# Halved first loads, statistics summed in one piece and two queues for the last stores, in a kernel of linear attention and a gated feed-forward layer

## The chip, the cores and the metric

The kernel runs on one core of a Trainium2 chip. TensorE does the matrix products, VectorE (DVE) and ScalarE (ACT) the elementwise work, GpSimd (POOL) some elementwise work and the issue of the loads, SyncE (SP) the issue of most stores. The metric is the device time in microseconds (us); the span of a profile is 1.7 to 1.8 us shorter than the time of the same execution.

## The reference, cut to what matters

```python
kv  = einsum('bhsd,bhse->bhde', k, v)              # 8 batches, 8 heads, 576 rows, 64 columns
out = einsum('bhsd,bhde->bhse', q, kv)
x   = out / sqrt(mean(out*out, -1) + 1e-6) * g_norm    # then 4608 tokens x 512
h   = x @ w_in                                      # 512 x 1024
solu = h * softmax(h)
ln  = (solu - mean(solu)) / sqrt(var(solu) + 1e-6) * g_ln
y   = ln @ w_out                                    # 1024 x 512
```

## The kernel before

The 4608 tokens are worked in nine chunks of 512: the first 512 rows of each batch (chunks 0 to 7), and the last 64 rows of all eight (chunk 8, its q in the tile `q_last`). Each piece of work is put on a list with its engine, its length and a rank, and a greedy planner fixes the order in which the pieces are written out for each engine.

A chunk's way: load k, v, q; product k·v ("kv"), copied into the tile `kvd`; q turned by TensorE and copied; product q·kv ("o"); square, a product that sums over the heads ("s"), logarithm and exponential on ScalarE give x; then eight groups of four products with w_in ("h"), an exponential and a multiplication for each (`u = h * exp(h)`), and eight groups with w_out ("out"). The softmax's denominator cancels in the normalization, so three sums per token are enough: of u, of its square and of exp. TensorE forms them, VectorE turns them by a transpose, and a small product ("stat") puts them where they are used.

The loads of a chunk are whole, and twelve products on zeros keep TensorE busy before the first kv:

```python
plan.add("warm2", "pe", 2.6, -9.0, lambda: warm(12), [("qT_mm", 0, 1)], first=[("s", "warm2")])
...
def load_kv(name, src, b):
    t = T[name, b] = tile_of((name, b), [S // 6, H, 6, D], BF16)
    nc.gpsimd.dma_start(t.rearrange("p h i d -> p h (i d)"), src[b].rearrange("h (p i) d -> p h (i d)", i=6))
```

The sums are three pieces for the planner, with 32-column weights on a quarter of the array:

```python
def sums(c, part):
    ...
    for n in range(n_src):
        j = n % 4
        nc.tensor.matmul(T["sum", c][32 * j:32 * j + 32, :], stat_sel[:, i, :], src[:, n, :], ...,
                         tile_position=(0, 32 * j), ...)
...
for part in range(3):
    plan.add(("sums", c, part), "pe", (0.5, 0.5, 0.25)[part], r + 0.1 + 0.02 * part, ...)
```

Stores are issued by SyncE. Those of chunk 8 have the batch, 8, as the slowest dimension of what they write:

```python
def store(c, m):
    ...
        dst = out.rearrange("(b s) d -> b s d", b=B)[:, 512:S, :].rearrange("b (p j) d -> j b p d", j=4)
    nc.sync.dma_start(dst[j], T["ob", c, m][:, :])
```

The softmax here doesn't subtract the row's maximum and nothing guards it: scores larger than these inputs give would overflow.

Of the kernel before, what the change touches and what calls it, by code (L numbers as in the profile page):

```python
# [18 lines left out]
class Plan:  # L19
# [13 lines left out]
    def order(self):  # L33
        free, done, queue, lanes = {}, {}, 0.0, []
        held = {tag: [] for tag in self.bufs}
        waiting = {n: set(p[4]) for n, p in self.pieces.items()}
        behind = {}
        for n, needs in waiting.items():
            for m in needs:
                behind.setdefault(m, []).append(n)  # L40
        ready = [n for n, needs in waiting.items() if not needs]
        order = []
        while ready:
            best = None
            for n in ready:
                engine, length, rank, fn, needs, first, load = self.pieces[n]
                t = max([free.get(engine, 0.0)] + [done[m] for m in needs])
                for key in first:
                    old = held[key[0]]
                    if len(old) >= self.bufs[key[0]]:  # L50
                        last = self.users[old[-self.bufs[key[0]]]]
                        t = max([t] + [done.get(m, 1e9) for m in last])
                if load and len(lanes) >= 8:
                    t = max(t, lanes[-8])
                if t < 1e8 and (best is None or (t, rank) < best[:2]):
                    best = (t, rank, n)
            t, rank, n = best
            engine, length, rank, fn, needs, first, load = self.pieces[n]
            ready.remove(n)
            for key in first:  # L60
                held[key[0]].append(key)
            free[engine] = t + length
            done[n] = t + length + (0.2 if engine == "pe" else 0.12)
            if load:
                queue = max(queue, t + length + 1.0) + load
                done[n] = queue + 1.0
                lanes.append(done[n])
            order.append(fn)
            for m in behind.get(n, ()):
                waiting[m].discard(n)  # L70
                if not waiting[m]:
                    ready.append(m)
        assert len(order) == len(self.pieces)
        return order
# [3 lines left out]
def kernel(  # L78
# [33 lines left out]
    banks = {"h": 2, "out": 2, "o": 2, "s": 1, "misc": 1}  # L112
    bufs = {
        "k": 3, "v": 3, "q": 3, "qT": 4, "osq": 4, "lss": 2, "rst": 2, "oc": 2, "x": 2, "e": 4, "u": 2, "usq": 2, "es": 2,
# [43 lines left out]
    for i in range(3):  # L158
        nc.vector.memset(stat_sel[:, i, i:i + 1], 1.0 / 1024)

# [16 lines left out]
    plan.add("warm", "pe", 5.2, -9.0, lambda: warm(12), first=[("s", "warm")])  # L177
    for n, key in enumerate((("o_mm", 0, 1), ("s_mm", (0, 0, 0)), ("s_mm", (0, 1, 0)), ("s_mm", (0, 0, 1)), ("s_mm", (0, 1, 1)))):
        plan.add(("warm", n), "pe", 0.7, -9.0, lambda: warm(3, "misc"), [key], first=[("misc", "warm", n)])
    plan.add("warm2", "pe", 2.6, -9.0, lambda: warm(12), [("qT_mm", 0, 1)], first=[("s", "warm2")])  # L180
# [9 lines left out]
    plan.add("ident", "pool", 1.0, -1.75, make_ident)  # L190
# [3 lines left out]
    def load_kv(name, src, b):  # L194

        t = T[name, b] = tile_of((name, b), [S // 6, H, 6, D], BF16)
        nc.gpsimd.dma_start(t.rearrange("p h i d -> p h (i d)"), src[b].rearrange("h (p i) d -> p h (i d)", i=6))

    def load_q(b):
        t = T["q", b] = tile_of(("q", b), [128, H, 4, D], BF16)  # L200
        nc.gpsimd.dma_start(
            t.rearrange("p h j d -> p h (j d)"), q[b, :, 0:512, :].rearrange("h (p j) d -> p h (j d)", j=4)
# [15 lines left out]
    T["q", NC - 1] = q_last  # L218
    for b in range(B):
        at = b - 2.4 if b > 1 else (-2.0, -1.5)[b]  # L220
        behind = [] if b < 2 else [("x", (0, 1, 1))] if b == 2 else [("h_mm", b - 3, 2)]
        plan.add(("k", b), "pool", 0.75, at, lambda b=b: load_kv("k", k, b), behind, first=[("k", b)], load=3.0)
        plan.add(("v", b), "pool", 0.75, at + 0.01, lambda b=b: load_kv("v", v, b), behind, first=[("v", b)], load=3.0)
        plan.add(("q", b), "pool", 0.9, at + (0.1 if b else -0.1), lambda b=b: load_q(b), behind, first=[("q", b)], load=2.7)
        plan.add(("q_last", b), "pool", 0.6, 2.0 + 0.5 * b, lambda b=b: load_q_last(b),
                 [("h_mm", 2 + b // 2, 4 * (b % 2))], load=0.5)
    for half in range(2):
        plan.add(("w_in", half), "pool", 0.8, -1.8 + 0.01 * half, lambda half=half: load_w_in(half), load=2.7)
# [3 lines left out]
    def kv_mm(b):  # L232
        t = T["kv", b] = bank(("misc", "kv", b), [128, NP, D], FP32)
        for p in range(NP):
            for i in range(6):
                for hh in range(2):
                    h = 2 * p + hh
                    nc.tensor.matmul(  # L238
                        t[hh * 64:hh * 64 + 64, p, :], T["k", b][:, h, i, :], T["v", b][:, h, i, :],
                        start=(p == 0 and i == 0), stop=(i == 5), skip_group_check=True,  # L240
                    )

    def kv_copy(b, hh, z):

        dst, src = kvd[z * 64:z * 64 + 64, b, hh, :, :], T["kv", b][hh * 64:hh * 64 + 64, :, :]
# [13 lines left out]
    def qT_copy(c, hf):  # L259
        t = T["qT", c, hf] = tile_of(("qT", c, hf), [128, 4, 2, 128], BF16)  # L260
        nc.vector.tensor_copy(t[:, :, :, :], T["qTp", c, hf][:, :, :, :])  # L261

    def o_mm(c, hf, tag):
# [4 lines left out]
        for pp in range(2):  # L268
            for b in [c] if c < B else range(B):
                cols = slice(0, 128) if c < B else slice(16 * b, 16 * b + 16)  # L270
                for hh in range(2):
                    for z in range(2):
# [3 lines left out]
                            T["qT", c, hf][rows, 2 * pp + hh, :, cols], start=True, stop=True,  # L276
# [38 lines left out]
    for c in range(NC):  # L315

        r = {0: -1.7, 1: -0.9}.get(c, c - 1.6)
        w = {0: 0.7, 1: 0.8}.get(c, 1.0)
        if c < B:
            plan.add(("kv_mm", c), "pe", 1.15, r, lambda c=c: kv_mm(c), [("k", c), ("v", c)],  # L320
                     uses=[("k", c), ("v", c)], first=[("misc", "kv", c)])
            for hh in range(2):
                for z in range(2):
                    plan.add(("kv", c, hh, z), "act" if hh else "dve", 0.34, r + 0.05,
                             lambda c=c, hh=hh, z=z: kv_copy(c, hh, z), [("kv_mm", c)], uses=[("misc", "kv", c)])
        kvs = [("kv", b, hh, z) for b in ([c] if c < B else range(B)) for hh in range(2) for z in range(2)]
        for hf in range(2):
            loads = [("q", c)] if c < B else [("q_last", b) for b in range(B)]
            qtag = "h" if c == 0 and hf else "misc"
            plan.add(("qT_mm", c, hf), "pe", 0.5, (r + w * (0.1 + 0.1 * hf)) if c else -2.0, lambda c=c, hf=hf, tag=qtag: qT_mm(c, hf, tag),  # L330
                     ["ident", *loads], uses=[("q", c)] if c < B else [], first=[(qtag, "qT", c, hf)])
            plan.add(("qT", c, hf), "dve", 0.62, (r + w * (0.12 + 0.1 * hf)) if c else -2.0, lambda c=c, hf=hf: qT_copy(c, hf),
                     [("qT_mm", c, hf)], uses=[(qtag, "qT", c, hf)], first=[("qT", c, hf)])
            tag = "out" if c == 0 and hf else "o"
            plan.add(("o_mm", c, hf), "pe", 0.25 if c < B else 1.2, r + w * (0.35 + 0.5 * hf),
                     lambda c=c, hf=hf, tag=tag: o_mm(c, hf, tag), [("qT", c, hf), *kvs],
                     uses=[("qT", c, hf)], first=[(tag, c, hf, z) for z in range(2)])
# [112 lines left out]
    def stats(c):  # L450
        st = small.tile([128, 4, 3], FP32, name="st")
        nc.vector.tensor_copy(st[:, :, :], T["st", c][:, :, :])
        sq = small.tile([128, 4, 2], FP32, name="sq")
        nc.vector.tensor_tensor(out=sq[:, :, :], in0=st[:, :, 1:3], in1=st[:, :, 1:3], op=MUL)
        var = small.tile([128, 4], FP32, name="var")
        nc.vector.tensor_tensor(out=var[:, :], in0=st[:, :, 0], in1=sq[:, :, 0], op=SUB)
        T["vare", c] = small.tile([128, 4], FP32, name="vare")
        nc.vector.scalar_tensor_tensor(
            out=T["vare", c][:, :], in0=sq[:, :, 1], scalar=1e-6 * d_ff * d_ff, in1=var[:, :], op0=MUL, op1=ADD
        )  # L460
# [35 lines left out]
    def store(c, m):  # L496
# [5 lines left out]
        nc.sync.dma_start(dst[j], T["ob", c, m][:, :])  # L502

    for f in range(NF):
        plan.add(("w_mean", f), "pe", 0.25, 0.2 + 0.05 * f, lambda f=f: w_mean(f),
                 ["w_out", "g_mean"] + ([("w_mean", f - 1)] if f else []), uses=[] if f == 0 else [("out", "mean")],
# [3 lines left out]
    for c in range(NC):  # L510
        r = c + 1
        parts = [[("u", c, f) for f in range(NF)], [("usq", c, f) for f in range(NF)], [("es", c, n) for n in range(NF // 2)]]
        for part in range(3):
            plan.add(("sums", c, part), "pe", (0.5, 0.5, 0.25)[part], r + 0.1 + 0.02 * part,
                     lambda c=c, part=part: sums(c, part),
                     parts[part] + ((parts[1] + parts[2] if c < NC - 1 else []) if part == 0 else [("sums", c, part - 1)]),
                     uses=[(("u", "usq", "es")[part], c)] + ([("misc", "sum", c)] if part else []),
                     first=[] if part else [("misc", "sum", c)])
        plan.add(("turn", c), "dve", 0.62, r + 0.14, lambda c=c: sums_turn(c), [("sums", c, 2)],
# [5 lines left out]
        for m in range(4):  # L525
# [9 lines left out]
            plan.add(("store", c, m), "sp", 0.6, r + (2 * m + 3) / 8, lambda c=c, m=m: store(c, m),  # L535
# [34 lines left out]
```

## Time and profile before

| | before |
|---|---|
| time, first three runs | 223.78 us median (223.01 to 224.43) |
| the profiled execution | 220.5 us, span 218.7 us |
| kv of chunk 3 starts | 56.10 us |
| TensorE's last product ends | 207.68 us |
| span after it | 11.05 us |

The profiled execution is faster than each of the three timed ones. The page's row of the granted TensorE clock, in 40 slices of 5.5 us, in tenths:

```profile
PEclk9699999999999999999999999999999999999995
```

And two lines of TensorE's timeline at the start (start, length, line, operation, tile, shape, count, idle before and what ended it):

```profile
7.40 0.99 PE L257 MATMUL misc_ps<-ident,q_sb 128*128 128x128 bf16 x8 [2.04 <-DMA q_sb<-in_q_dram]
...
9.04 3.67 PE L175 MATMUL s_ps<-zeros 128*128 128x512 bf16 x12
```

TensorE waited 2.04 us for q, and then its clock was 0.5 from about 7.4 to 10.9 us. In this stretch it turns q and works through the twelve products on zeros, and then stands for v until 13.72. So here the slow stretch costs nothing.

### The profile page before, as it was taken

The numbers are of one execution on the slowest core, as the hardware profiler recorded it, in microseconds if no ns is written. First come the engines' busy times: TensorE is split into PE (matmuls) and PEld (weight loads), VectorE is DVE, ScalarE is ACT, GpSimd is POOL, SyncE is SP. The second block draws the span as 40 slices with busy tenths as digits, with TensorE's granted clock in tenths as the row PEclk, the third lists the DMA queues.
The fourth block names the chain that finished last, engine by engine and source line by source line (L and its number), as shares of the span: only waits on it lengthen the run. The fifth ranks groups of instructions, "written<-read, shape, count | busy, mean of one in ns | idle before, by whom it ended". The sixth has DMA issues, their size and how long they took to land.

```text
span 218.7 us, 4197 instructions
## 1 busy us (share of the span) xinstructions
PE 188.8 (86%) x1669; PEld 85.8 (39%) x1695; DVE 137.7 (63%) x249; ACT 133.8 (61%) x227; POOL 131.8 (60%) x136
## 2 busy tenths in 40 slices
PE   7669796588999989999998999899999999999900
PEld 2434343243553444344435444443453444344300
DVE  1326564896777596669648675966785675493240
ACT  2019577757866877784977679586849685342000
POOL 8606299529479727984695584468466477485000
PEclk9699999999999999999999999999999999999995
DMA  5999999994992697289719940311032022013023
GB/s 53 187 201 205 230 361 201 201 189 53 201 210 60 94 193 185 63 109 221 190 13 189 224 115 4 109 48 51 0 119 76 3 96 96 0 64 125 6 69 124
DMA packets 30483, 27.01 MB, mean 123 GB/s; under 512 B 2304, under 2 KB 24832, under 8 KB 30464
## 3 DMA queue, kind: packets, MB, share of 16 engines
q0 software_dynamic: 24112, 17.30, 52.1%
q1 hardware_dynamic: 6352, 9.44, 12.6%
q8 instruction: 13, 0.21, 0.4%
q14 instruction: 6, 0.05, 0.1%
HBM read 32.51 MB, written 9.44 MB: 192 GB/s over the span
## 4 chain that ended last, share of the span: by engine, by line
PE 63%; DVE 14%; ACT 9%; DMA 5%; issue 4%; POOL 1%; DVEq 1%; POOLq 0%; ACTq 0%
PE out_ps L487 24%; PE h_ps L365 23%; PE misc_ps L429 6%; DMA v_sb<-in_v_dram 5%; PE misc_ps L257 3%; PE s_ps L295 3%; PE o_ps L274 3%; DVE u_sb L380 3%; DVE x_sb L310 2%; DVE ob_sb L494 2%; DVE kvd L247 2%; DVE w_out_sb L478 2%; ACT lss_sb L299 2%; ACT e_sb L373 2%; ACT osq_sb L289 2%
## 5 line engine op out<-in xcount | busy, mean ns | idle before, releaser
L365 PE MATMUL h_ps<-x_sb,w_in_sb 128*128 128x512 bf16 x273 | 71.7, 379 | 5.1 <-DVE x_sb L310 3.1
L391 POOL TENSOR_TENSOR usq_sb<-u_sb 128x512 bf16<-128x512 bf16 x58 | 59.9, 1040 | 23.1 <-DVE u_sb L380 23.1
L373 ACT ACTIVATE e_sb<-h_ps,zero_t 128x512 f32<-128x512 f32 x72 | 49.2, 684 | 37.7 <-PE h_ps L365 35.7
L487 PE MATMUL out_ps<-w_out_sb,u_sb 128*128 128x512 bf16 x262 | 67.1, 380 | 2.4 <-DVE ob_sb L494 1.1
L397 POOL TENSOR_TENSOR es_sb<-e_sb 128x512 bf16<-128x512 f32 x36 | 45.7, 1269 | 37.4 <-ACT e_sb L373 37.3
L380 DVE TENSOR_TENSOR u_sb<-h_ps,e_sb 128x512 bf16<-128x512 f32 x72 | 48.9, 684 | 22.9 <-ACT e_sb L373 22.6
L365 PEld LDWEIGHTS <-w_in_sb 128*128 128x128 bf16 x288 | 26.4, 98 | 34.7 <-issue 7.7
L487 PEld LDWEIGHTS <-u_sb 128*128 128x128 bf16 x288 | 26.1, 98 | 34.5 <-issue 7.0
L494 DVE TENSOR_SCALAR ob_sb<-out_ps,rstd 128x512 f32<-128x512 f32 x34 | 24.9, 743 | 11.7 <-PE out_ps L487 10.2
L310 DVE SCALAR_TENSOR_TENSOR x_sb<-o_ps,g_rep,rst_sb 128x512 bf16<-128x512 f32 x34 | 25.4, 746 | 6.5 <-ACT rst_sb L303 6.4
L303 ACT ACTIVATE rst_sb<-lss_sb,zero_t 128x512 f32<-128x512 f32 x36 | 25.8, 722 | 0.6
L299 ACT ACTIVATE lss_sb<-s_ps,eps_t 128x512 f32<-128x512 f32 x34 | 23.2, 683 | 1.9 <-PE s_ps L295 1.9
L289 ACT ACTIVATE osq_sb<-o_ps,zero_t 128x512 bf16<-128x512 f32 x33 | 21.1, 684 | 3.7 <-PE o_ps L274 2.7
L249 ACT CAST kvd<-misc_ps 64x256 bf16<-64x256 f32 x16 | 5.9, 368 | 16.7 <-DVE kvd L247 16.3
L295 PE MATMUL s_ps<-osq_sb,head_mean 128*128 128x512 bf16 x34 | 12.9, 380 | 0.7 <-ACT lss_sb L299 0.7
L257 PE MATMUL misc_ps<-ident,q_sb 128*128 128x128 bf16 x120 | 9.5, 224 | 3.8 <-DMA q_sb<-in_q_dram 2.0
L257 PEld LDWEIGHTS <-q_sb 128*128 128x128 bf16 x128 | 8.8, 103 | 8.8 <-issue 3.5
L438 DVE STREAM_TRANSPOSE sumT_sb<-misc_ps 128x512 f32<-128x512 f32 x9 | 6.4, 713 | 9.1 <-PE misc_ps L429 9.1
L261 DVE COPY qT_sb<-misc_ps 128x1024 bf16<-128x1024 bf16 x17 | 11.6, 679 | 0.4 <-PE misc_ps L257 0.4
L389 ACT ACTIVATE usq_sb<-u_sb,zero_t 128x512 bf16<-128x512 bf16 x14 | 10.1, 722 | 2.6 <-DVE u_sb L380 2.6
L274 PE MATMUL o_ps<-qT_sb,kvd 64*64 64x32 bf16 (+1 forms) x248 | 8.7, 229 | 2.2 <-DVE kvd L247 1.1
L247 DVE CAST kvd<-misc_ps 64x256 bf16<-64x256 f32 x16 | 6.6, 414 | 5.3 <-PE misc_ps L238 3.0
(60 smaller groups left out, 133.0 us busy)
## 6 DMA issues: line engine op xcount, KB each, us to landing
out_dram<-ob_sb SPq DMA_DIRECT2D x36, 256.0 KB, 3.1
k_sb<-in_k_dram POOLq DMA_DIRECT2D x8, 576.0 KB, 7.3
v_sb<-in_v_dram POOLq DMA_DIRECT2D x8, 576.0 KB, 9.8
q_sb<-in_q_dram POOLq DMA_DIRECT2D x8, 512.0 KB, 12.6
w_out_f<-in_moe_w_out_dram POOLq DMA_DIRECT2D x1, 2048.0 KB, 26.1
w_in_sb<-in_moe_w_in_dram POOLq DMA_DIRECT2D x2, 512.0 KB, 13.8
q_last<-in_q_dram POOLq DMA_DIRECT2D x8, 64.0 KB, 3.1
g_rep<-in_g_norm_dram SPq DMA_DIRECT2D x2, 0.2 KB, 2.3
```

The lines of the kernel that those rows point to most:

```text
L257: nc.tensor.transpose(t[:, h, y, :], src, ident[:, :])
L289: nc.scalar.activation(out=t[:, :], in_=T[("o", *i)].rearrange("p a b c -> p (a b c)"), func=AF.Square, bias=zero_t[:, :])
L299: nc.scalar.activation(out=t[:, :], in_=T["s", i][:, :], func=AF.Ln, bias=eps_t[:, :])
L303: nc.scalar.activation(out=t.rearrange("p a b c -> p (a b c)"), in_=T["lss", i][:, :], func=AF.Exp, scale=-0.5, bias=zero_t[:, :])
L310: nc.vector.scalar_tensor_tensor(out=T["x", c][:, 2 * hf:2 * hf + 2, z], in0=T["o", c, hf, z][:, :, :, :], scalar=g_rep[:, :], in1=T["rst" ...
L365: nc.tensor.matmul(t[:, :], w_in_sb[:, dt, f * 128:(f + 1) * 128], T["x", c][:, dt].rearrange("p a b c -> p (a b c)"), start=(dt == 0), st ...
L373: nc.scalar.activation(out=T["e", c, f // 2][:, f % 2, :], in_=T["h", c, f][:, :], func=AF.Exp, bias=zero_t[:, :])
L380: nc.vector.tensor_tensor(out=T["u", c][:, f, :], in0=T["h", c, f][:, :], in1=T["e", c, f // 2][:, f % 2, :], op=MUL)
L391: nc.gpsimd.tensor_tensor(out=dst, in0=src, in1=src, op=MUL)
L397: nc.gpsimd.tensor_tensor(out=T["es", c][:, n, :], in0=e[:, 0, :], in1=e[:, 1, :], op=ADD)
L487: nc.tensor.matmul(T["acc", c, m][:, :], T["u", c][:, f, m * 128:(m + 1) * 128], w_out_sb[:, f, :], start=(f == 0), stop=(f == NF - 1),)
L494: nc.vector.tensor_scalar_mul(out=t[:, :], in0=T["acc", c, m][:, :], scalar1=T["rstd", c][:, m:m + 1])
```

## The change

The intent is to start earlier, to spend less on the statistics and to shorten the end. The loads of chunks 0 and 1 are split by halves of the heads, each half with its own kv and o. The sums become one piece. The last four stores alternate between the queues of SyncE and ScalarE. Nine groups of three products on zeros take the place of the twelve. The planner charges 0.1 for a change of tiling on TensorE, and 2.5 for a store to land. The four small VectorE operations of the statistics are regrouped, still four. Turning q by a transfer is written, but its list of chunks is empty. Smaller parts are not in the cut below: the planner counts every tile that one piece fills, the turned q has one tile for both halves (three whole tiles instead of four halves), the products that average w_out wait for chunk 1's o, and the first loads have a new order. The core of the diff, cut:

```diff
+            if engine == "pe":
+                tiling = n[0] if n[0] in ("kv_mm", "o_mm", "sums", "st_mm") else "full"
+                length += 0.1 if mode.get(engine, tiling) != tiling else 0.0
+                mode[engine] = tiling
...
-            done[n] = t + length + (0.2 if engine == "pe" else 0.12)
+            done[n] = t + length + {"pe": 0.2, "sp": 2.5}.get(engine, 0.12)
...
+    XBAR = ()
...
+    for n in range(9):
+        plan.add(("warm", "s", n), "pe", 0.65, 8.0, lambda: warm(3), ["warm"], first=[("s", "warm", n)])
-    plan.add("warm2", "pe", 2.6, -9.0, lambda: warm(12), [("qT_mm", 0, 1)], first=[("s", "warm2")])
...
+    def heads(c):
+        return (slice(0, 4), slice(4, 8)) if c < 2 else (slice(0, 8),)
...
+        nc.gpsimd.dma_start(
+            T[name, b].rearrange("p h i d -> p h (i d)")[:, hs], src[b].rearrange("h (p i) d -> p h (i d)", i=6)[:, hs]
         )
...
-        nc.sync.dma_start(dst[j], T["ob", c, m][:, :])
+        (nc.scalar if c == NC - 1 and m % 2 else nc.sync).dma_start(dst[j], T["ob", c, m][:, :])
...
-        for part in range(3):
-            plan.add(("sums", c, part), "pe", (0.5, 0.5, 0.25)[part], r + 0.1 + 0.02 * part, ...
+        plan.add(("sums", c), "pe", 1.2, r + 0.1, lambda c=c: [sums(c, part) for part in range(3)], sum(parts, []),
```

## The prediction

> **What bounds the kernel now.** I read the page first (share of each engine, slices, chain), then TensorE's timeline at the start, in a middle chunk and at the end, then the waits and the rate of transfers.
>
> The page:
>
> ```profile
> span 218.7 us, 4197 instructions
> PE 188.8 (86%) x1669; PEld 85.8 (39%) x1695; DVE 137.7 (63%) x249; ACT 133.8 (61%) x227; POOL 131.8 (60%) x136
> PE   7669796588999989999998999899999999999900
> PE 63%; DVE 14%; ACT 9%; DMA 5%; issue 4%; POOL 1%; DVEq 1%; POOLq 0%; ACTq 0%
> ```
>
> The third line has 40 slices of 5.5 us. From slice 12 (60 us) to slice 38 (207 us) TensorE is full; before that it has holes, and after that it is empty. So there are three places to win: the first 60 us, TensorE's own work per chunk, and the last 11 us.
>
> The start, in TensorE's timeline (start, length, tile, idle before and its end):
>
> ```profile
> 13.72 0.95 PE L238 MATMUL misc_ps<-v_sb,k_sb 96*64 96x64 bf16 x48 [1.01 <-DMA v_sb<-in_v_dram]
> 23.15 2.11 PE L365 MATMUL h_ps<-x_sb,w_in_sb 128*128 128x512 bf16 x8 [1.43 <-DVE x_sb L310]
> 39.74 0.95 PE L238 MATMUL misc_ps<-v_sb,k_sb 96*64 96x64 bf16 x48
> 42.88 0.59 PE L365 MATMUL h_ps<-x_sb,w_in_sb 128*128 128x512 bf16 x2 [1.65 <-DVE x_sb L310]
> ```
>
> The first kv product waits for v to 13.7, the first h for x to 23.15, and chunk 1's first h stands for x again until 42.88.
>
> A middle chunk, where the sums of the statistics come in three parts:
>
> ```profile
> 89.82 1.03 PE L365 MATMUL h_ps<-x_sb,w_in_sb 128*128 128x512 bf16 x4
> 90.78 0.61 PE L429 MATMUL misc_ps<-u_sb,stat_sel 128*32 128x512 bf16 x8
> 91.33 0.41 PE L274 MATMUL o_ps<-qT_sb,kvd 64*64 64x256 bf16 x8
> 91.67 0.62 PE L429 MATMUL misc_ps<-usq_sb,stat_sel 128*32 128x512 bf16 x8
> 93.18 0.40 PE L429 MATMUL misc_ps<-es_sb,stat_sel 128*32 128x512 bf16 x4
> 99.33 0.61 PE L257 MATMUL misc_ps<-ident,q_sb 128*128 128x128 bf16 x8 [0.48 <-ACT kvd L249]
> ```
>
> 512-column products start 0.216 us apart ((1.03 - 0.38) / 3), so four h products from 89.82 end at 90.68, and the tiled sums start 0.10 later.
>
> The end, in the timeline and in windows of 1 us (the last three numbers: TensorE's clock, share of the 16 DMA engines, GB/s):
>
> ```profile
> 206.46 0.25 PE L443 MATMUL misc_ps<-sumT_sb,fold 128*32 128x12 f32 x8
> 206.64 1.04 PE L487 MATMUL o_ps<-w_out_sb,u_sb 128*128 128x512 bf16 x4
> 208.24 1.41 DVE L494 TENSOR_SCALAR ob_sb<-out_ps,rstd 128x512 f32<-128x512 f32 x2 [0.69 <-ACT rstd L466]
> ...
> 196.00:197.00 1.00, 1.00 (x6) 0.48 (x5) 0.91 (x2) 0.13 (x2) 1.00 (x2) 1.00 0.98 367
> 213.00:214.00 1.00, 0.00 (x0) 0.00 (x0) 0.00 (x0) 0.00 (x0) 0.00 (x0) 0.50 0.51 184
> ```
>
> The scaling of the last four blocks starts only when rstd is there, 0.7 after TensorE's last product (207.5), and ends at 210.96; the span ends at 218.7. An ordinary store moves 367 GB/s with all engines; the four last ones, alone from 210 on, move 184 with half of them.
>
> **The Trainium skill.** "TensorEngine Tiling (Array Packing)", Key Properties, says that changing the tiling mode drains TensorE. The trace agrees: 0.09 to 0.10 us at each entry from full to tiled products (90.68 to 90.78 above), and none between two tilings (91.33, 91.67). "DMA: Bandwidth & Descriptors", "Why a DMA increments its semaphore by 16 and not by 1", says that a transfer uses the largest k up to 16 that divides the slowest dimension of both sides, and for the hardware queues the lowest-numbered k engines. The last stores have 8 as slowest dimension; half the share and half the rate agree with k = 8. The same page, "Issuing engines are not separate DMA queues", says that a second issuing engine saves only the time to issue. No run yet shows that.
>
> **The change, part by part.**
>
> *q by TensorE.* The DMA turning is written but its list is empty. The before kernel also turns all nine chunks on TensorE. Worth 0.
>
> *Halves.* Byte counts, as the two-byte copies that the rate column counts: q of a chunk 128x8x256x2 = 524 KB, k and v 96x8x384x2 = 590 KB each, w_in twice 524, w_out (four bytes) 2097. The loads run as one stream: 1 us windows from 3 to 12 us sum to 1516 KB, so q0+k0+v0 (1704 KB) are over at 12.9, and the product starts at 13.72: 0.7 us to land. The changed order is q0a, k0a, v0a: 852 KB, over at 8.6, landed about 9.3. Their kv, copies and o product follow at 9.3 to 11.7. The second half still needs all 1704 KB, about 13.5. From there: half a kv product 0.44, four kvd copies at about 0.3 (0.37 to 0.42 for double width), o product 0.35, then on ScalarE one waiting log and exponential of the first half, square, log, exponential, log, exponential (0.6 each): x whole at about 21.1, not 23.75. But TensorE's order now has chunk 1's first kv half before the first h: 1704 + 1049 (w_in) + 590 = another 1639 KB at 200, so 21.8. First h about 22.3, 0.9 earlier.
>
> Then chunk 1: its second halves land near 26 (k, v) and 27.4 (q); o near 29; four square/log/exponential sets with five e's between at 0.6 give x near 36 instead of 42.8. This isn't all kept. Bytes do not change, so chunk 2's v lands as before at 39.55 (issue 19.45 + 20.1) and q at 42.0 (20.22 + 21.8), and the new TensorE order puts kv(2), a mean product and the turning of q(2) before h(1,2). So TensorE has done two h groups of chunk 1 by 42.0 and then waits for q. Also the eight w_center multiplications (0.68 apart) come after that on VectorE: two at 43.0, a q copy, six to 49.7 (48.2 before). Then: second out group 50.0, another to 50.9, stat product 51.3, o(2,1) until x(2,0,1) frees its bank at 51.9, to 52.35, out 53.2, square sums 53.4, kv(3) 54.4, and h(1,4) at 54.4. Before, it is at 57.2 after the same four out groups, with one 0.2 square-sum product more done. Gain 2.6, and 0.1 for a first transfer issued sooner: **2.7 us**.
>
> *Statistics in one piece.* Tiled entries per chunk: before sums, sums, stat, kv, o = 5; after sums, stat with o, kv, o = 4. That saves 0.1. A square-sum product (0.22) now lies between kv and the next q turning, which waits about 0.6 for the kvd copies: up to 0.22 more. Against it, the stat product now stands behind one h group (0.86) and a transpose of 0.11 + 0.72 plus its signal: up to 0.15 lost. I take 0.2 a chunk over seven: **1.4 us**. The short VectorE chain has four operations of 0.17 before and four after; 0.1 at most.
>
> *The end.* Before, the stat product comes 1.04 before TensorE ends (207.5); now twelve products follow it: 0.18 + 2.6 = 2.8. Stat to first scaled block is 2.5 (206.46 to 208.98). So that block is ready 0.3 before TensorE ends, not 1.5 after: 1.8. The stores are 4 x 262 KB at 188 = 5.6 us, longer than the four scalings (2.7), so they stay bound by eight engines on either queue; filling the dips at the start of the stream gives about 0.5. **2.3 us**.
>
> Sum 2.7 + 1.4 + 2.3 = 6.4; 223.78 - 6.4 = 217.4 us.
>
> **Rivals.** *The start is hidden:* chunk 2's q lands at 42.0 whatever is done and w_center ends later than before. Then only 3.7 remains, 220.1. For it: the same bytes, a stream without holes to 42. Against: at 42.0 two h groups are done where before half of one was. *The stat product waits:* VectorE is 63% busy, and a transpose behind one 0.7 operation costs 0.3 to 0.5 a chunk on TensorE, which eats the middle gain: 219 to 220. For it: a 0.21 wait of this kind at 172.26. Against: in the new order the operation before the transpose belongs to an h group that ends 2.4 earlier. *Two queues double the store rate:* 5.6 becomes 2.8, 215 in all. Against: the k = 8 reading. *The early gain grows:* if x(1) at 36 lets later chunks run ahead, 214.
>
> **Range and chances.** The end is the surest part (1.8 of it is order alone), the start the least (0 to 5), the middle 0 to 2.5. Together 213.8 to 221.0. Over 2% means under 219.3, for which 4.5 of the 6.4 must come: 0.76. Within 2%: 0.22. Slower: 0.02, as no engine gets work that lies on its path.
>
> **What would show it.** First kv near 9.3 and first h near 22.3; q(2) turned near 42; h(1,4) near 54.4; middle chunks 19.7 apart at the sums, not 19.91 (90.78 to 110.69); the last stat product about 2.8 before TensorE's end; last stores still at half share near 188 GB/s. It would be wrong if x(1) came after 39, if stat products wait on the transpose by more than 0.3, or if the last stores show a share near 1.

## The result, and the profile after

The changed kernel takes 213.43 us (median of 4 runs, 213.30 to 214.51), against 223.39 us (4 runs, 222.10 to 224.43) for the kernel before. The ratio is 0.9565, with a 95% interval from 0.9513 to 0.9617. A ratio here is the mean time of one kernel's fast runs over that of the other's of the same rounds, so it is not quite the ratio of the medians. The result is faster, as the prediction thought likely, but it lies below its range of 213.8 to 221.0, and 4.0 us below its 217.4.

The page of the changed kernel:

```profile
span 212.7 us, 4283 instructions
PE 193.0 (91%) x1710; PEld 87.9 (41%) x1710; DVE 135.7 (64%) x255; ACT 132.8 (62%) x231; POOL 136.0 (64%) x142
PE   7599997889999999999999999999999999999910
PEclk9969999999999999999999999999999999999985
```

TensorE's row, in slices of 5.3 us, shows fewer holes in the first ten and hardly any later, where the row of before has an 8 every few slices. This profile is of the slowest of the kernel's executions (214.51 us), while the profile of before is of its fastest. Profile against profile, the span falls by only 6.0 us; median against median, the time falls by 10.0.

The start, in TensorE's timeline:

```profile
9.89 0.57 PE L272 MATMUL misc_ps<-v_sb,k_sb 96*64 96x64 bf16 x24 [2.10 <-DMA v_sb<-in_v_dram]
...
15.55 0.81 PE L186 MATMUL s_ps<-zeros 128*128 128x512 bf16 x3
16.29 0.57 PE L272 MATMUL misc_ps<-v_sb,k_sb 96*64 96x64 bf16 x24
...
18.18 0.81 PE L186 MATMUL misc_ps<-zeros 128*128 128x512 bf16 x3 [0.36 <-ACT kvd L284]
...
24.48 1.04 PE L420 MATMUL h_ps<-x_sb,w_in_sb 128*128 128x512 bf16 x4
```

The first half of v lets kv start at 9.89 (predicted near 9.3). The second half's kv stands behind a filler at 15.55, and a filler at 18.18 stands in front of the second o product. The first h comes at 24.48 (predicted 22.3), chunk 1's x is whole at about 40.1 (predicted 36), q of chunk 2 is turned from 43.90 (predicted 42), and the fifth h group of chunk 1 starts at 56.12 (predicted 54.4; 57.2 before).

A middle chunk:

```profile
97.30 0.61 PE L292 MATMUL misc_ps<-ident,q_sb 128*128 128x128 bf16 x8 [0.17 <-DVE kvd L282]
...
98.61 1.03 PE L541 MATMUL out_ps<-w_out_sb,u_sb 128*128 128x512 bf16 x4
99.61 0.61 PE L292 MATMUL misc_ps<-ident,q_sb 128*128 128x128 bf16 x8
...
107.93 0.61 PE L484 MATMUL misc_ps<-u_sb,stat_sel 128*32 128x512 bf16 x8
108.37 0.60 PE L484 MATMUL misc_ps<-usq_sb,stat_sel 128*32 128x512 bf16 x8
108.81 0.39 PE L484 MATMUL misc_ps<-es_sb,stat_sel 128*32 128x512 bf16 x4
109.13 1.04 PE L420 MATMUL h_ps<-x_sb,w_in_sb 128*128 128x512 bf16 x4
```

The three sums take 1.20 us from 107.93 to the next h. Two parts of eight are now 0.44 apart; in the kernel before, a part of eight takes 0.55 (90.78 to 91.33) even before another tiled product. The wait for `kvd` before the first turning of q is 0.17, where it was 0.48. The period from kv of chunk 3 to kv of chunk 7, divided by four, is 19.47 us ((133.09 - 55.23) / 4) against 19.95 before ((135.88 - 56.10) / 4).

The end:

```profile
199.71 0.25 PE L498 MATMUL misc_ps<-sumT_sb,fold 128*32 128x12 f32 x8
...
201.31 1.41 DVE L548 TENSOR_SCALAR ob_sb<-out_ps,rstd 128x512 f32<-128x512 f32 x2 [0.69 <-ACT rstd L520]
```

TensorE's last twelve products run from 199.90 to 202.66, so the stat product comes 2.95 before the end (predicted 2.8), and the first block's scaling of about 0.7 is over by 202.0 (predicted 0.3 before TensorE's end, measured about 0.6). In windows of 1 us (the last three numbers are the clock, the share of the 16 DMA engines and GB/s):

```profile
205.00:206.00 1.00, 0.00 (x0) 0.00 (x0) 0.00 (x0) 0.00 (x0) 0.00 (x0) 0.65 0.53 193
206.00:207.00 1.00, 0.00 (x0) 0.00 (x0) 0.00 (x0) 0.00 (x0) 0.00 (x0) 0.50 0.50 184
207.00:208.00 1.00, 0.00 (x0) 0.00 (x0) 0.00 (x0) 0.00 (x0) 0.00 (x0) 0.50 0.53 133
```

The share is still a half, and the rate falls to 133 and 137 after 207. The span goes on for 10.04 us after TensorE's end, against 11.05.

Three marks cut the span into three parts, before and after: the start to kv of chunk 3 (56.10, 55.23), from there to TensorE's end (151.58, 147.43), and what follows (11.05, 10.04). The gains are 0.9, 4.15 and 1.0. The prediction had 2.7, 1.4 and 2.3. That the sums, 6.0 and 6.4, lie near each other is luck: no single term agrees, and the two profiles are of executions of unlike kinds.

### The profile page after: what moved, and what is told of

Same layout as the page of the kernel before. It is cut to its first block, busy times and chain, and to the rows that moved or that the text cites. A ratio compares the mean times of both kernels' runs of the same rounds, so it can differ in the third digit from the quotient of the medians.

```text
span 212.7 us, 4283 instructions
## 1 busy us (share of the span) xinstructions
PE 193.0 (91%) x1710; PEld 87.9 (41%) x1710; DVE 135.7 (64%) x255; ACT 132.8 (62%) x231; POOL 136.0 (64%) x142
## 4 chain that ended last, share of the span: by engine, by line
PE 67%; ACT 11%; DVE 10%; DMA 3%; issue 3%; POOL 1%; DVEq 0%; POOLq 0%; ACTq 0%
PE out_ps L541 24%; PE h_ps L420 23%; PE misc_ps L484 4%; PE misc_ps L292 4%; DMA v_sb<-in_v_dram 3%; PE o_ps L317 3%; ACT rst_sb L346 3%; ACT e_sb L428 3%; PE s_ps L338 3%; DVE x_sb L353 2%; DVE kvd L282 2%; DVE ob_sb L548 2%; ACT lss_sb L342 2%; PE misc_ps L272 2%; DVE w_out_sb L532 2%
## 5 line engine op out<-in xcount | busy, mean ns | idle before, releaser
L420 PE MATMUL h_ps<-x_sb,w_in_sb 128*128 128x512 bf16 x288 | 74.0, 379 | 0.5 <-DVE u_sb L435 0.4
L541 PE MATMUL out_ps<-w_out_sb,u_sb 128*128 128x512 bf16 x272 | 69.6, 380 | 0.4 <-DVE w_out_sb L532 0.3
L435 DVE TENSOR_TENSOR u_sb<-h_ps,e_sb 128x512 bf16<-128x512 f32 x72 | 49.4, 687 | 27.4 <-ACT e_sb L428 27.4
L541 PEld LDWEIGHTS <-u_sb 128*128 128x128 bf16 x288 | 26.7, 98 | 33.9 <-issue 4.9
L353 DVE SCALAR_TENSOR_TENSOR x_sb<-o_ps,g_rep,rst_sb 128x512 bf16<-128x512 f32 x32 | 23.9, 748 | 9.6 <-ACT rst_sb L346 9.6
L332 ACT ACTIVATE osq_sb<-o_ps,zero_t 128x512 bf16<-128x512 f32 x31 | 20.2, 681 | 3.7 <-PE o_ps L317 3.6
L284 ACT CAST kvd<-misc_ps 64x256 bf16<-64x256 f32 (+1 forms) x20 | 6.5, 326 | 13.6 <-DVE kvd L282 13.4
L186 PE MATMUL s_ps<-zeros 128*128 128x512 bf16 x39 | 12.3, 447 | 1.5 <-DVE zeros L153 1.2
L217 POOL DMA_DIRECT2D q_sb<-in_q_dram x10 | 8.7, 873 | 1.8 <-DMA v_sb<-in_v_dram 1.0
```

Of the source, the lines that this page charges most:

```text
L332: nc.scalar.activation(out=t[:, :], in_=T[("o", *i)].rearrange("p a b c -> p (a b c)"), func=AF.Square, bias=zero_t[:, :])
L353: nc.vector.scalar_tensor_tensor(out=T["x", c][:, 2 * hf:2 * hf + 2, z], in0=T["o", c, hf, z][:, :, :, :], scalar=g_rep[:, :], in1=T["rst" ...
L420: nc.tensor.matmul(t[:, :], w_in_sb[:, dt, f * 128:(f + 1) * 128], T["x", c][:, dt].rearrange("p a b c -> p (a b c)"), start=(dt == 0), st ...
L435: nc.vector.tensor_tensor(out=T["u", c][:, f, :], in0=T["h", c, f][:, :], in1=T["e", c, f // 2][:, f % 2, :], op=MUL)
L541: nc.tensor.matmul(T["acc", c, m][:, :], T["u", c][:, f, m * 128:(m + 1) * 128], w_out_sb[:, f, :], start=(f == 0), stop=(f == NF - 1),)
```

## The experiments

Fourteen runs were made, two of them of the kernel before itself; all but e11, a single execution, share their rounds with the kernel before. All results were correct. e1 to e8 ran on one chip, e9 to e12 on a second, e13 and e14 on a third; the chip of the first pair is not on record. The kernel before had medians of 223.5 to 223.6, 222.95 and 223.11 on the three, so a difference of medians across chips can be off by about 0.6 us. "kv(3)" is the start of chunk 3's kv product in that kernel's profile.

| run | median us (range) | ratio to before, 95% | kv(3) | clock |
|---|---|---|---|---|
| changed kernel | 213.43 (213.30 to 214.51) | 0.9565 (0.9513 to 0.9617) | 55.23 | 0.975 |
| e1_before_again | 222.18 (221.39 to 224.47) | 0.9967 (0.9913 to 1.0022) | 60.03 | 0.958 |
| e2_one_queue | 213.05 (212.45 to 213.97) | 0.9551 (0.9506 to 0.9596) | 54.15 | 0.987 |
| e3_sums_parts | 219.83 (219.73 to 220.58) | 0.9854 (0.9808 to 0.9899) | 55.50 | 0.984 |
| e4_whole_loads | 216.40 (216.17 to 217.54) | 0.9706 (0.9663 to 0.9749) | 58.08 | 0.979 |
| e5_old_warm | 216.58 (215.47 to 217.02) | 0.9687 (0.9639 to 0.9736) | 58.51 | 0.968 |
| e6_before_fill | 223.82 (222.68 to 225.94) | 1.0016 (0.9966 to 1.0065) | 61.42 | 0.966 |
| e7_stores16 | 210.29 (210.03 to 211.23) | 0.9431 (0.9389 to 0.9473) | 54.42 | 0.991 |
| e8_stores16_one | 210.80 (210.08 to 211.30) | 0.9440 (0.9399 to 0.9482) | 55.02 | 0.996 |
| e9_before_sums_one | 216.17 (215.91 to 216.92) | 0.9707 (0.9661 to 0.9754) | 61.01 | 0.953 |
| e10_best_a | 212.16 (211.27 to 212.41) | 0.9522 (0.9480 to 0.9565) | 56.61 | 0.983 |
| e11_before_look | 221.02 (one run, state unknown) | none | 56.52 | 0.977 |
| e12_before_fillers | 222.28 (220.39 to 223.14) | 0.9973 (0.9919 to 1.0027) | 55.79 | 0.986 |
| e13_charge_early | 211.72 (210.81 to 212.50) | 0.9494 (0.9448 to 0.9539) | 54.08 | 0.988 |
| e14_charge_early_16 | 208.06 (207.62 to 208.84) | 0.9331 (0.9286 to 0.9375) | 55.55 | 0.989 |

### The kernel before, again: e1_before_again and e11_before_look

No edit in either.

> The kernel before, unchanged, to see its spread. Its profile that I predicted from has a span of 218.7 us, while its timed runs have a median of 223.4; the changed kernel's span of 212.7 belongs to 214.5. Theory A (the profile of before was an unusually fast execution): a second profile has a span of 220 to 223 us, and its extra 2 to 3 us lie in one place, probably in the first 60 us where TensorE has holes and the granted clock can fall to 0.5. Theory B (the timed runs carry an overhead that no profile shows): the span is again 218.5 to 219, at timed runs of 223. In both the ratio to before is 1.00.

> Kernel before once more, unchanged, for a third profile of it. Theory (the profile that I predicted from was of the fastest execution, where the half clock fell into a wait): the span goes with the start of chunk 3's kv, at 56.1 for a span of 218.7 and 60.0 for 222.7, and kv(3) to the end of the span stays 162.6 to 162.7; a time of 223.4 would show kv(3) near 59 and half clock after 16 or after 44. Rival (the spread lies in the middle or in the stores): kv(3) to the end differs by over 1 us from 162.6.

The profile of e1 is of an execution of 224.47 us, with a span of 222.7, 4.0 more than the profile that the prediction was made from. Its row of the clock:

```profile
PEclk9995999979999999999999999999999999999975
```

And its timeline:

```profile
14.34 0.95 PE L238 MATMUL misc_ps<-v_sb,k_sb 96*64 96x64 bf16 x48 [2.89 <-DMA v_sb<-in_v_dram]
...
46.70 1.68 PE L487 MATMUL out_ps<-w_out_sb,u_sb 128*128 128x512 bf16 x4
48.18 1.91 PE L365 MATMUL h_ps<-x_sb,w_in_sb 128*128 128x512 bf16 x4
```

The low clock has moved. In the early profile it lay before the wait for v. Here TensorE ran the twelve fillers at full clock, so it was through sooner, stood 2.89 us for v, and had a clock of 0.5 from 17 to 23 us, when the work for the first x waits for it. It fell once more from 47 to 50, after a wait of 1.65 for x, which stands in the first profile too (42.88) and lowers nothing there. The four out products at 46.70 take 1.68; in the first profile the same four take 1.03:

```profile
44.16 1.03 PE L487 MATMUL out_ps<-w_out_sb,u_sb 128*128 128x512 bf16 x4
```

kv(3) comes at 60.03 instead of 56.10, 3.93 later, which is the whole difference of the spans. Not all of it is the clock: v of chunk 0 landed 0.62 later (14.34 for 13.72). By the first h the delay is 2.55 (25.70 for 23.15), and 1.38 more come after it. From kv(3) to the end of the span are 162.60 us in the first profile (218.7 - 56.10), 162.67 in e1 and 162.68 in e11 (219.2 - 56.52). So what differs between executions of the kernel before lies in its first 60 us. e11 was an execution of 221.02 us, again with the low clock early (8 to 11 us) and kv(3) at 56.52; its expectation of kv(3) near 59 spoke of an execution of 223.4, which this one wasn't.

The mean clock of an execution says the same without a profile. Of 38 executions of the kernel before with a recorded clock in the fast state, the ten with 0.974 or more took 220.50 to 222.43 us, the ten from 0.968 to 0.971 took 221.39 to 223.21, and the eighteen from 0.955 to 0.963 took 222.96 to 224.47. The base profile stands in the first group and is the fastest of all; the median of the base runs, 223.4, stands in the third.

Why the same wait lowers the clock in one execution and not in another can be read from the kept traces. In the sixteen profiles, each of the 14 stretches at half clock before the end of the work lasts 3.41 us or twice that. Cut into steps of 3.41 us from such a stretch, the step before the fall has TensorE busy for 1.37 us in the first profile (4.07 to 7.48) and for 1.24 and 1.50 in e1 (12.81 to 16.22, 43.53 to 46.94). The wait of 1.65 for x lies within one step in e1. In the first profile the border of two steps falls into it, the step from 41.61 to 45.02 is busy for 1.89, and the clock stays. In all profiles, steps at full clock with up to 1.51 us of work were followed by half clock each time (12 of 12), steps with 1.89 or more never, and between 1.61 and 1.87 both occurred. So in these runs the clock followed how much TensorE did in a step, and the steps lie elsewhere in each execution. This is read from the traces; no run was made to test it, and the ends of products in a trace are modelled.

### The queues: e2_one_queue

```diff
-        (nc.scalar if c == NC - 1 and m % 2 else nc.sync).dma_start(dst[j], T["ob", c, m][:, :])
+        nc.sync.dma_start(dst[j], T["ob", c, m][:, :])
```

> The changed kernel with all stores on the one queue, nothing else. My theory (the last stores run on eight engines whichever queue issues them): at most 0.6 us slower, 213.4 to 214.0. Rival (two queues double the rate): 2 to 3 us slower, 215.5 to 216.5.

The time is 213.05, and its range overlaps that of the changed kernel. In the profile the span goes on for 9.15 us after TensorE's end instead of 10.04, and from 204 to 209 us the rates are 193, 188, 129, 193 and 180 GB/s. Theory and rival had both expected it slower than with two. The second queue gained nothing: in the two profiles it is 0.9 slower, which the times (213.43 against 213.05) neither confirm nor rule out. The other profiles on eight engines agree: 9.69 to 10.33 in the five with two queues (the changed kernel, e3, e4, e5, e13), 9.15 and 9.34 in the two with one and the same order at the end (e2, e9).

### The statistics in parts, and in one piece alone: e3_sums_parts and e9_before_sums_one

e3 is the changed kernel with the three pieces of before; e9 is the kernel before with the one piece:

```diff
-        for part in range(3):
-            plan.add(("sums", c, part), "pe", (0.5, 0.5, 0.25)[part], r + 0.1 + 0.02 * part, ...
+        plan.add(("sums", c), "pe", 1.2, r + 0.1, lambda c=c: [sums(c, part) for part in range(3)], sum(parts, []), ...
```

> The changed kernel with the sums in three parts again. Theory from the two traces: a block of sums costs 1.20 us in one piece and 0.55 + 0.55 + 0.34 in three, and each part has its entry of 0.10, so 0.4 us a chunk over seven chunks and about 3 us in all: 216 to 217. What I had predicted for this part: 1.4 us, 214.8. Rival (other waits fill the room): 213.4 to 214.

> Kernel before, only the sums of the statistics put in one piece. The order of TensorE shows that the last stat product then has twelve products behind it, as in the changed kernel. Theory (the one piece is the main part of the change): period of a middle chunk, kv(3) to kv(7) over four, near 19.4 instead of 19.91 to 19.95, seven or eight periods give 3.5 to 4.5 us, and the earlier last stat product 1 to 1.8 more: 217.5 to 219, ratio 0.975 to 0.98, and kv(3) still at 56 to 60. My prediction's size (0.2 a chunk and 1.8 at the end): 220 to 220.5, ratio 0.985 to 0.987. Rival (the piece pays only in the changed order, since the placing of the q turning matters): within 1 % of before.

Undoing the one piece costs the changed kernel 6.4 us (219.83 - 213.43). This is twice the 3 that was expected from the sums alone. Its period rises from 19.47 to 20.29, and the wait before the first turning of q from 0.17 to 0.81:

```profile
99.00 0.61 PE L292 MATMUL misc_ps<-ident,q_sb 128*128 128x128 bf16 x8 [0.81 <-DVE kvd L282]
```

The piece alone takes 6.8 us off the kernel before (222.95 to 216.17), more than the 4 to 5.5 expected. The period is 19.04 ((137.16 - 61.01) / 4), 0.91 less than 19.95. From kv(3) to TensorE's end are 144.75 us, 6.83 less than before. The rest of the span is 9.34 instead of 11.05, since the last stat product has twelve products behind it here as well. Some of both is lost at the start, which fell into the slow kind in all six executions (clocks 0.953 to 0.967).

This gives more than the whole change has in the middle (4.15), so some other part of the change has to give 2.7 back. e9's timeline shows where:

```profile
101.16 1.03 PE L487 MATMUL out_ps<-w_out_sb,u_sb 128*128 128x512 bf16 x4
102.08 0.61 PE L257 MATMUL misc_ps<-ident,q_sb 128*128 128x128 bf16 x8
...
104.25 1.03 PE L365 MATMUL h_ps<-x_sb,w_in_sb 128*128 128x512 bf16 x4
105.11 0.61 PE L257 MATMUL misc_ps<-ident,q_sb 128*128 128x128 bf16 x8
105.65 0.41 PE L274 MATMUL o_ps<-qT_sb,kvd 64*64 64x256 bf16 x8
```

After the first turning of q come h, out and another h before the second turning, which follows at once (104.25 + 4 x 0.216 = 105.11). In the changed kernel only h and out lie between, and the second turning comes 1.00 after an out group of 0.86, so it waited 0.14. The first turning waited as well there (0.33 after the end of the out group, and 0.05 in e9), and before one s product 0.09 was lost. In these two chunks that is 0.51 (0.28, 0.14 and 0.09), and their periods differ by 0.49.

### The planner's charge: e13_charge_early and e14_charge_early_16

```diff
-                length += 0.1 if mode.get(engine, tiling) != tiling else 0.0
+                length += 0.1 if mode.get(engine, tiling) != tiling and t < 50.0 else 0.0
```

e13 is the changed kernel with this edit, which leaves TensorE's order as it is up to chunk 3 and gives the middle chunks the order of e9. e14 has the edit and the stores of e7, told below.

> Changed kernel, only that the scheduler charges 0.1 for a change of tiling in the first 50 us of its plan alone. TensorE's order is then the same as in the changed kernel up to chunk 3, and in the middle chunks the same as in the run with only the sums in one piece: one more h group before the second q turning. Theory (the charge made an order in which the q turnings wait for VectorE, which gives back 0.45 of 0.92 a chunk): period kv(3) to kv(7) over four 19.04 instead of 19.47, time 213.4 - 0.43 x 7 = 210.4, 209.8 to 211.2. Rival (the 0.45 comes from the q tile of both halves or from the statistics' operations on VectorE, which this keeps): period 19.4 to 19.5 and 213.0 to 213.6.

> The same edit on the kernel with the last stores to sixteen partitions (two queues, 210.3). Theory: the two gains lie in different parts and add: 210.3 - 3.0 = 207.3, 206.8 to 208.2, ratio to before near 0.93. Rival (the middle isn't changed by the order): 210.0 to 210.6.

The period is 19.05 in both profiles. So the charge is what gave back 0.43 a chunk, and the parts that e13 keeps from the change (one tile for both halves of q, the regrouped statistics) cost nothing there. The time of e13, 211.72, is 0.5 above what was expected: two of its six executions were at 210.8 to 210.9, three at 212.2 to 212.5. From kv(3) to TensorE's end are 144.78 us, as in e9 and 2.65 less than in the changed kernel; that its median gained only 1.7 is not explained by a profile. e7 and e14 differ by the same edit: there the stretch is 2.31 shorter (147.98 to 145.67) and the median falls by 2.23, which agree. e14, at 208.06, is the fastest kernel.

### The halves: e4_whole_loads

```diff
     def heads(c):
-        return (slice(0, 4), slice(4, 8)) if c < 2 else (slice(0, 8),)
+        return (slice(0, 8),)
     def group(c, hf):
-        return hf if c < 2 else 0
+        return 0
```

> The changed kernel with k, v and q of chunks 0 and 1 loaded and attended whole, as before. From the landmarks (fifth h of chunk 1 at 57.2 us before, 56.1 after) the halves gave only about 1.1 us: 214.3 to 214.9. My prediction's 2.7 us would give 216. A rival in which the halves are what makes the start steady from run to run (before has 222.1 to 224.4): 216.5 to 218, with a larger spread.

Without the halves the changed kernel takes 3.0 us more (216.40 - 213.43), twice what the landmarks of the slow profile had let expect (0.9 to 1.5) and just below the rival's 216.5. The first kv waits for v to 14.46 again, and kv(3) comes at 58.08.

### The fillers: e5_old_warm, e6_before_fill, e12_before_fillers and e10_best_a

e5 is the changed kernel with the twelve products in place of the nine groups. e6 is the kernel before with 24 products instead of twelve, and eight more before chunk 1's x. e12 is the kernel before with the nine groups:

```diff
 e5, and e12 the other way round
-    for n in range(9):
-        plan.add(("warm", "s", n), "pe", 0.65, 8.0, lambda: warm(3), ["warm"], first=[("s", "warm", n)])
+    plan.add("warm2", "pe", 2.6, -9.0, lambda: warm(12), [("qT_mm", 0, 1)], first=[("s", "warm2")])
 e6
+    plan.add("warm2", "pe", 2.6, -9.0, lambda: warm(24), [("qT_mm", 0, 1)], first=[("s", "warm2")])
+    plan.add("warm3", "pe", 0.0, -9.0, lambda: warm(8), [("s_mm", (1, 1, 1))], first=[("s", "warm3")])
```

> The changed kernel with the nine groups of filler products taken out and the one group of twelve of the kernel before put back. Clock theory (the second profile of before lost 4 us where the granted clock fell to half after idle stretches at the start; the fillers keep TensorE busy there): 214.5 to 217 us, with a spread over 1.5 us and a mean clock below 0.975. Rival (the fillers stand in the way, two of them delay the first attention by about 2 us in all): 212 to 213, spread under 1 us.

> The kernel before with twelve more filler products while v of chunk 0 is awaited and eight after the last square sum of chunk 1; the order of everything else is the same. Clock theory: 220 to 221.5 us, spread under 1.5 us, mean clock 0.975 or more, and the third product with k and v over 2 us earlier than in the slow profile (60.0). Rival (the spread has another cause, such as the transfers): 223 to 224 with the spread of 3 to 4 us as before.

> Kernel before with the change's nine filler groups in place of the twelve products, nothing else. Theory (the fillers of the change win because they keep the clock in the first 25 us): clock 1.00 from 12 to 24 and kv(3) near 56, time 220 to 221.5, spread within 1.5. Rival (fillers are only worth something with halves, because whole loads make waits too long to fill): 223 to 225 and half clock somewhere from 8 to 24. The undoing in the changed kernel cost 3.1.

In e5 the clock is 0.5 from about 11 to 17 us, the twelve products in a row take 4.83 there, and the second half's kv stands behind them until 17.86; the kernel takes 3.1 us more. So the halves and the fillers need each other: with either missing, about 3 of the gain are gone (e4 and e5). No run of the changed kernel lacks both.

e6 was badly made. q landed late, the clock fell before the 24 products, they took 7.44 us, and kv of chunk 0 waited for them until 17.41. It says only that one long block of fillers at half clock delays what it is to protect.

e12 kept the clock at 1.00 in every window of the profiled execution up to 56 us, and kv(3) came at 55.79. But its other executions took 221.5 to 223.1 at clocks of 0.966 to 0.978, so alone the fillers are worth no more than the interval (0.9919 to 1.0027), less than expected. Which wait drops the clock in its slower executions no profile shows.

e10 removes five older filler groups from the kernel of e7, since two fillers stood in the way at the start:

```diff
-    for n, key in enumerate((("o_mm", 0, 1), ("s_mm", (0, 0, 0)), ... ("s_mm", (0, 1, 1)))):
-        plan.add(("warm", n), "pe", 0.7, -9.0, lambda: warm(3, "misc"), [key], first=[("misc", "warm", n)])
```

> Last stores to sixteen partitions on two queues, as measured at 210.3, without the five old filler groups in the misc bank, so that kv of chunk 0's second half comes before the filler that waited for a log. Theory (two fillers block by about 0.6 each on the path to the first h): first h near 23.5 instead of 24.5, but q of chunk 2 still lands near 42, so at most 1 us is kept: 209.3 to 210.3. Rival (the clock falls without them before the first h): 211 to 213 with half clock between 18 and 24. Rival (the load stream sets the start): 210.0 to 210.6.

```profile
22.42 1.01 PE L418 MATMUL h_ps<-x_sb,w_in_sb 128*128 128x512 bf16 x2 [2.13 <-DVE x_sb L351]
...
24.14 1.74 PE L418 MATMUL h_ps<-x_sb,w_in_sb 128*128 128x512 bf16 x4
```

The first two products of h, on the first half of the heads, start at 19.70 already; the next two stand 2.13 us for the rest of x, which comes 2.1 sooner than the first h of the changed kernel (24.48). The clock was 0.5 from 22.2 to 25.6, so that four h products took 1.74 instead of 1.03, and again from about 39 to 43. The time is 212.16 against 210.29, on another chip; by the ratios 0.9522 against 0.9431, whose intervals do not meet. The rival of the clock was right, and the fillers that look in the way pay for themselves.

### Stores on sixteen engines: e7_stores16 and e8_stores16_one

The rows of chunk 8 are laid over the partitions the other way round, so that the slowest dimension of a store is 16 (the rows) and not 8 (the batches). e7 uses two queues, e8 one.

```diff
-            q_last[16 * b:16 * b + 16].rearrange("p h j d -> p h (j d)"),
+            q_last[b::8].rearrange("p h j d -> p h (j d)"),
-                cols = slice(0, 128) if c < B else slice(16 * b, 16 * b + 16)
+                cols = slice(0, 128) if c < B else slice(b, 128, 8)
-            dst = ....rearrange("b (p j) d -> j b p d", j=4)
+            dst = ....rearrange("b (p j) d -> j p b d", j=4)
```

> The changed kernel with the last chunk laid out so that its stores have 16, not 8, as slowest dimension; two queues as changed. Engine-count theory: the stores run at a share near 1 and over 300 GB/s, the stretch from TensorE's end to the span's end falls from 10.0 to about 7.5 us: 210.5 to 211.3. Rival (the store tail is bound by the writes' landing, not by engines): 213 to 213.5, share still near 0.5. The last chunk's products with columns 8 apart may cost up to 0.5 us.

> The same layout with all stores on one queue. If two queues only get in each other's way (with eight engines one queue was 0.4 us faster in the medians): 0 to 0.4 us faster than the same layout on two queues. Rival (with 16 engines the time to issue is the bound): 0.3 to 1 us slower.

The windows of e7:

```profile
204.00:205.00 1.00, 0.00 (x0) 0.00 (x0) 0.00 (x0) 0.00 (x0) 0.00 (x0) 0.72 1.05 375
205.00:206.00 1.00, 0.00 (x0) 0.00 (x0) 0.00 (x0) 0.00 (x0) 0.00 (x0) 0.50 0.84 293
```

The rate is twice that of the changed kernel, the share near one, and the span ends 5.9 us after TensorE's end (202.41 to 208.3). The time falls by 3.1 us, to 210.29. With one queue it is 210.80, with overlapping ranges: here too the second queue is worth nothing that these runs resolve. The dimension counts, not the queue.

The layout has a price. The o products of chunk 8 now read and write columns eight apart. Here they are contiguous (e13) and strided (e14):

```profile
154.67 0.69 PE L317 MATMUL o_ps<-qT_sb,kvd 64*64 64x32 bf16 x64
```

```profile
156.14 1.13 PE L317 MATMUL o_ps<-qT_sb,kvd 64*64 64x32 bf16 x64
```

That is 0.44 more, twice, and 0.9 is lost from kv(3) to TensorE's end (145.67 against 144.78); between the changed kernel and e7 it is 0.55 (147.98 against 147.43). Whether the reading or the writing costs it was not tested. Without it, about 207.2 would be left for e14 (an estimate, 208.06 - 0.9).

## Why the prediction was right or wrong

**The base.** The first step that failed is the one that was not written down: taking the marks of one profile for those of the median. The sum of 6.4 was worked out within an execution of 220.5 us and subtracted from 223.78. With 162.65 from kv(3) to the end (the mean of the three profiles), a span of 221.6 (the median 223.4 less 1.8) means kv(3) at about 58.95; the profile had 56.10. The changed kernel's median of 213.43 means a span of 211.6 and, with 157.47 from kv(3) to the end (212.7 - 55.23), kv(3) at about 54.1, as e2 and e13 have it (54.15, 54.08). Both are estimates from these numbers. So the start gained about 4.8, where the prediction had 2.7. Between the two profiles in which the half clock costs nothing (56.10 and e2's 54.15) the gain is 2.0; the other 2.8, as far as e1 shows it, is mostly half clock that a median execution of the kernel before has in its way and one of the changed kernel has not. The prediction was right to call the start its least sure term, and the row of the clock was on its page, but the step that reads the start never asked where the low clock lay, or whether it always lies there.

**The start.** "Half a kv product ... x whole at about 21.1 ... First h about 22.3": here the step missed that filler groups stand between these pieces. The first h came at 24.48. Two things explain it: in this profile the clock was 0.5 from about 10.7 to 14 us, and at full clock, in e2, the first h comes at 23.45; and in e10, without the older fillers, the whole of x is there for h at 22.42, near the prediction's 22.3. Chunk 1's x at 40.1 was past the 39 that the prediction named as a sign of error (39.0 in e2). The later marks came within 2: q turned at 43.90 for 42, the fifth h group at 56.12 for 54.4; at full clock, in e2, within 0.8 (42.80 and 55.03). The rival that the start is hidden fell (e4: 3.0 lost without the halves). The prediction's diff reading gave the fillers no line of their own, and they carry as much as the halves (e5: 3.1).

**The middle.** "That saves 0.1" and "I take 0.2 a chunk" was the worst-sized term, and the largest part of the miss: the one piece is worth 0.91 a chunk (e9). Two things were left out. The prediction counted what entering a tiled product costs and not what leaving one costs: between full products, a lone part of eight takes 0.65, 0.10 to enter and 0.55 to go on, against 0.44 within the block. Its "none between two tilings" was a misreading of the same line: the 0.55 from 90.78 to 91.33 ends at a tiled product of another shape, and has the 0.11 in it. And with three parts the planner's order let the first turning of q stand for the copies of `kvd`, 0.81 in e3. From the lines shown, the first is about 0.35 a chunk (0.10 + 0.55 + 0.55 + 0.10 + 0.34 for the three parts before, 0.09 + 1.20 for the block), and the second 0.59 (the first turning starts 0.65 us after the end of the products ahead of it in the kernel before, 0.06 in e9). The sum of this estimate, 0.94, is near the 0.91. "The stat product waits" was given as the rival for the middle, and it fell: no such wait stands in the middle chunk's lines. What was lost came from a line read as bookkeeping, the charge for a change of tiling. The prediction does not mention it. It moved the second turning of q ahead of an h group and gave back 0.43 a chunk (e13). The period of 19.7 that was predicted lies nearer the measured 19.47 than to 19.04 only because two unseen effects of unlike sign stood against each other.

**The end.** The order's 1.8 was right: the span after TensorE's end falls by 1.7 in e9 and by 1.9 in e2, both with one queue. The 0.5 for the second queue failed: the changed kernel keeps 1.0 of 2.3. That eight engines bind the stores was right (e7), and the rival of a doubled rate by two queues fell.

**q by TensorE.** Worth 0, as the list is empty. No run tests it by itself; e13's period equals e9's with the new tile for q in it.

Together the gains are 4.8, 4.15 and 1.0, which is 9.95, against a measured 9.96 between the medians. This is no check: the middle and the end stand in the profiles, but the start was worked out from the medians, so the sum has to agree. Against the prediction the start gave 2.1 more, the middle 2.75 more and the end 1.3 less; with the 0.4 by which the base fell when its fourth run came in (223.78 to 223.39), this is the 4.0 between 217.4 and 213.4. What stays open is where the half clock lay in the slower executions of e12 and e13, of which no profile was taken, and the 1.0 of e13's middle gain that its median doesn't show.

## What to carry to other kernels

Before subtracting a gain from a median, check that the profile's own time is near that median, and look in the row of the granted clock for a stretch below full: where it lies can differ from one execution to the next, and its cost depends on what waits there. Count both edges of a tiled block on TensorE, and read a planner's cost constants as a change of order, not as bookkeeping: here one constant was worth 2.65 us in the profile of e13 and 1.7 to 2.2 in the medians (e13, e14), found only by running one part of the change alone. When a transfer runs at half rate, change the dimension that limits its engines before adding a queue.

## What the Trainium skill lacked or had wrong

- "TensorE: Matmul & The Clock Gate", Part 1, "What's actually happening": it says that a free-running window of about 3.4 us of idling halves the clock, that this varies by run, and that the ramp penalty is under 1% of a typical span. The runs agree with the halving (0.5 in the windows), with a window of that length (stretches of 3.41 and 6.83 us) and with the variation. It gives no share of busy time that still counts as idling: here TensorE was busy for 0.38 to 1.85 of the 3.41 us before each fall, and up to 1.51 the fall came each time. The figure for the ramp doesn't cover a clock that falls again: the profiles of one unchanged kernel differ by 4.0 of 222.7 us, 1.8%, all of it before kv(3), of which 0.62 is a later v.
- "TensorEngine Tiling (Array Packing)", "Key Properties": the drain has no figure there. It measured 0.10 at the entry and about 0.11 at the exit of a tiled block (0.55 for a part of eight against 0.44 within one), and the same 0.11 between two tilings.
- "DMA: Bandwidth & Descriptors", "Issuing engines are not separate DMA queues": the runs agree that a second issuer brings no gain (213.43 against 213.05, 210.29 against 210.80). It doesn't say that it may cost: on eight engines 9.69 to 10.33 us after TensorE's end in five profiles with two queues, and 9.15 and 9.34 in two with one; on sixteen engines 5.90 and 5.88.
- No page gives a figure for the cost of strided columns to a matrix product: 64 products of 32 columns took 1.13 us with a stride of eight in what they read and write, and 0.69 without.
